# A speech joint network on one core: a leading tile of 330 outputs, weight sums over PSUM and on GpSimd, and orders found anew

## The chip, the cores and the metric

The kernel runs on one core of one Trainium2 chip. The metric is the device time in microseconds. TensorE (PE) does the matmuls and writes PSUM, which has eight banks of 512 fp32 columns; VectorE (DVE) and ScalarE (ACT) read and write SBUF and PSUM; GpSimd (POOL) works on SBUF here; SyncE (SP) issues nearly all transfers.

## The reference

x is 2 x 4000 x 512 in bf16, the two convolutions have 5 taps of 512 x 512, g is 2 x 8 x 512.

```python
h = sum(einsum("btc,cd->btd", xp[:, i:i+T, :], w1[i]) for i in range(5))
h = gelu(h)[:, ::2, :]                       # 2000 rows a batch
f = sum(einsum("btc,cd->btd", hp[:, i:i+T1, :], w2[i]) for i in range(5))
f = gelu(f)[:, ::2, :]                       # 1000 rows a batch
fe, ge = f @ w_f, g @ w_g
j = tanh(fe[:, :, None, :] + ge[:, None, :, :])
return einsum("btud,dv->btuv", j, w_o)       # 2 x 1000 x 8 x 512
```

Only every second output of each convolution is needed.

## The kernel before

**The stages.** Outputs of conv1 are made in two ways. The first ones of batch 0, the *leading tile*, are made directly: for each of the 5 taps, the 4 blocks of 128 input channels and the 4 blocks `m` of 128 output channels one matmul (`direct`, 80 in all) over `2 * NA` columns. It needs x transposed: the first rows of x are loaded as they are (`xr`), transposed on TensorE against an identity (`turn`) and copied to SBUF (`xs`) by ScalarE and VectorE. Eight matmuls on zeros run ahead of that.

All other outputs are made in *triples*: a fast algorithm that makes three outputs in 9 products where the direct way takes 15. A triple over `n` columns makes 3n outputs with 9 x 4 x 4 = 144 matmuls of n columns. Its products are named `t2`, `tm`, `sm`, `t1`, `s1`, `t0`, `s0`, `ti`, `si`. Batch 0 has two triples of conv1 (`N3`, 266 columns each), batch 1 two of 334, and conv2 one of 334 for each batch. The inputs of a triple are the six phases of x (every sixth row, transposed by the transfer itself, `load_x6`, to `xq` and `xp`), doubled (`d0`, `d1`, `d2`) and subtracted from each other (`r0` to `r2`, and the steps that bear the products' names) in `Triple.step`. A `Unit` is one triple's work for one block `m`: `s1` to `s5` are the products with their copies and sums.

The triples need sums of the taps' weights. `w1part` makes them for conv1, per block `m`: `t = w0 + w4`, `v = t - w2`, `u = 4 w4 + w0 + 2 w2`; `u/3` and `v/3` go to `w1_x` (for `t2` and `tm`), `t + w2` to `w1_t` (for `t1`), and `w1 - w3`, `w1 + w3`, `2 w1` (for `sm`, `s1`, `s0`) for two blocks at a time. The sums are fp32 tiles in SBUF (`ssum`); VectorE adds, ScalarE scales.

After the convolutions come `w_f`, `w_g`, the tanh on ScalarE and the joint product with `w_o` in 15 rounds (`Seven`: seven products of halved blocks for eight), with copies out of PSUM (`evict`), sums before them (`Seven.sums`, on VectorE or GpSimd) and stores.

**The order of the work.** Each operation is recorded with its engine, its tiles and a cost (`Plan.op`); `Plan.flex` records one that either of two engines can do. The order of each engine's operations is written out in `ORDER`, two characters an operation, and this also settles which engine does a flexible one. `Plan.edges` derives from the tiles who waits for whom; across engines these are semaphore waits. Each engine works strictly in its order, so what waits holds up all behind it.

**The transfers.** SP issues `xr`, then the taps 0 and 4 in parts, 2, 1 and 3, then six transposing loads for each triple. Some weight loads wait until an earlier load has landed (`gate`, an index into `came`).

The helpers record every operation, so the profile has their lines: `tt` (L398), `act` (L404), `mm` (L412), `stt` (L518), `turn` (L496, L505), `load_w` (L430), `load_x6` (L445), `load_w1` (L458), `evict` (L834, L835), `Seven.sums` (L903), `shared` (L1009).

Of the kernel before, what the change touches and what calls it, by code (L numbers as in the profile page):

```python
# [12 lines left out]
P = 128  # L13
# [50 lines left out]
class Op:  # L64
# [18 lines left out]
        "PyPePfPzQMP-Q0Q3Q4QNQCQDQIQJQFQGQPQQQTQUQXQYQbQeQfQi"),
    "act": (
        "080h0m1U0r1x1W1a1z1Z251Y2b1q271K2m1L2M1-1j2U1t2x1l1M1O332d2R1N3E2g2f2X2u2_3Z3B3H3R2h3h413c2r3K3s3M4K3x3f4C4V3p3y3w38"
        "494F4b3m3W3v4i5V5D464t4Y4P4S4y4d5C574q4w5z5B4n6E5A5g5154685d6V6g786j6v6G6M6a5j65795S6B5a745T627I7A7b6d7s5x7z7T717N6_"
        "7W7j7m5q6T7Q5w778D8d7u7g828O8B886s6t7p6S8X8-8L858o8Y9A8W9G8I8R8i8l9N7G948r9I976m9b9V9D9e9S8z9p9_9rA69YAcAXA8AFAtAdAP"
        "AfAMAeAhASAnBOAVB8BuB9AgBgCFCECs9wB7CGCqB-CJC2CCCrCDCeCwChDQCtDPDRFJDDD-CpE0DGDgEaDnFHCXEbE3D6FxFFFGFID_FwEMEFEZEPGS"
        "FyEpFNF2FYFKG_FCF5FhFzIWFkG-GIGVFvI0IVJ2GpGRGgGsHDJVH2J_HXI2IYHMHPI6I1IXIaJ-IMICIjJ6IdJ3ItI3IZJMIwJWJZK_JfK2JpKTJsNN"
        "KILSKdKRK-KnL2KUKyKqLwL8LVLILRLlL_NqKSLxM4MTMEMwMtMjMHKzMQNsN0MPMmNDNLNRMsOPNhNwNXNkNtNMOfOMNOODNrOpP6OLOiPJOoP9PPPZ"  # L90
        "PkQBPcPqP_Q1QOQHQRQgQdQk"),
    "dve": (
        "000j0o0p1R1S1v1T1V1X231w1u212Z1_1y24221b2a261d1c1Q1e1g1f1P1h1i1k28202p1m2P2Y362c1n2Q2q372e1o302i2k2j2-3U3I3V313J3L3k"
        "3P3z3l3O3N4H3-444I3_4N454Z4l4G4m4a4O4c4-4f4e504g5m5E5G5F5k5Y6D6J6F6C5l5Z5P6Y6l6L6K6Z605Q615N5O5t5p6I7C6H7D7Y6y7B5R5u"
        "6z7L7M7Z6P7q5o7X6Q5r7E6k5s5v7r7e6N806O7t7f6R816p7v6n7w6o6q7x6r8G7F8H8b8g8Z8h8u928t939H8a9F9h9f9Q9l9j9R9g8s9k9J9E9i9n"
        "9y9K9-A09mADA3A7AAA1AEAJ9uAHAOAL9vB5B69LAkAYAZBPAbAuBQAvBCAqA_BjBVBIBFBvB1BYBcBmBLByCaBpCMCPBsCZClC8CzCbCVDUCSD0CWD8"
        "DkDXEyEGEzEHD3DqDMDaE6DdDyDuEqDzEtErGCE9EkECEeEvFbEwEVEhEnFEF9FQExGjFtG6G0FTFaFWG3FqGBG9GYGLGbGPGiHHIGHlHIGyGeHFH5Hi"
        "HBHdH8HkHrHaHgHTI9H_HuIHIoJGIPIFITIgJHIpImJCJ9J0JcJFJjKDJkJiJPJTK5JyKXK8KBKaKgKPKLKjKkLDM8KwLbLfM9L5LBLPLuLYLLM1LeLo"
        "M7MAMBMdN4MLMZMWMzNAMqMcNHNUN3OZNdNbO4NcO5NaO3NzNoOAOVO0OsOSOyOvOHOmPDOYO-PMP2PTPuP3PUPvPSPnPgPtQ5QEQKQVQZQcQj"),
    "pool": (  # L100
        "01020304050s0t0u2A0v0w0x295n8VAaBSAwBRAxBwCYDjBxD9D7DhDiE-DAE_EJEsEIFcEuFeGkFdGlGDHGGFGEHmIIGmHoHJHnJIInIqIJJJKCJlKF"
        "KhKEJmLCKiLFLgLELiLhMfMeN5MgN6N7NeO6O7OaOcObP0P1PWPVPwPx"),
    "sp": (
        "0607090A0B0C0D0E0F0G0H0I0J0K0L0M0N0O0P0Q0R0S0T0U0V0W0X2B2C2D2E2F2G2H2I2J2K5H5I5J5K5L5M8S8T8UB2BZBdC3C4C5C9CiCmDHDIDJ"
        "DNDrDvEQERESEWF6FAFlFmFnFrGMGQGtGuGvGzHQHUHvHwHxH-IQIUIxIyIzJ1JQJUJtJuJvJzKMKQKrKsKtKxLMLQLpLqLrLvMIMMMNMOMnMrNENINJ"
        "NKNlNpOEOIOJOKOjOnPAPEPFPGPdPhQ2Q6Q7Q8QLQSQWQaQh"),
# [178 lines left out]
def bass_standalone__seq2seq_rnn_t_joint__speech_kernel(  # L285
# [25 lines left out]
    NA, N3 = 204, (266, 266)  # L311
# [9 lines left out]
    with ExitStack() as es:  # L321
# [33 lines left out]
        xq = [Buf(nc, f"xq{i}", [6, NK, (288, 288)[i]], BF16, v.end - v.bytes) for i, v in enumerate((xs[1], w2_sb))]  # L355
# [108 lines left out]
        def load_xq(i, ph):  # L464
            o = load_x6(xq[i], 0, ph, 2 * NA // 3 + i * N3[0] - 2, 0, -(-(N3[i] + 3 - i) // 16) * 16)
            if (i, ph) in ((0, 4), (0, 0)):
                o.wire = 1.050 if ph else 2.520

        lo, hi, al = slice(0, 2), slice(2, NK), slice(0, D)
        for i, part, gate in ((0, (lo, al), None), (0, (hi, al), None), (4, (slice(0, NK), slice(0, D // 2)), None),  # L470
                              (4, (slice(0, NK), slice(D // 2, D)), 0), (2, None, 1), (1, None, 3), (3, None, 5)):
            load_w1(i, part, gate)
        for ph in (4, 0, 2, 1, 3, 5):
            load_xq(0, ph)
# [14 lines left out]
        def turn(rt, pp, rs, bk):  # L489
# [8 lines left out]
            pl.op("pe", fn, (xr[rt].rows(0, n), ident[:]), (pv,), k * (0.2 if rt else 0.275))  # L498
# [41 lines left out]
        w13 = {0: 2, 2: 4}  # L540

        def w1part(m, part):
            sl = slice(m * P, (m + 1) * P)
            w = lambda i: w1_sb[i, :, sl]
            if part == "s":
# [8 lines left out]
                stt("dve", u, w(2), 2.0, u)  # L554
                act(w1_x[1, :, sl], u, ACT.Copy, scale=1.0 / 3.0)
                tt("dve", v, t, w(2), sub)
                act(w1_x[0, :, sl], v, ACT.Copy, scale=1.0 / 3.0)
                tt("dve", w1_t[2, :, sl], t, w(2), add)
# [3 lines left out]
        class Triple:  # L562
# [14 lines left out]
            def step(self, which):  # L577
                z, r = self.z, self.r
                E = self.n + 2
                if which[0] == "d":  # L580
                    i = int(which[1])
                    act(r(i, n=E), z(2 * i - 2, 0, E) if i else z(4, -1, E), ACT.Copy, scale=2.0)
# [3 lines left out]
                elif which == "next":  # L586
                    act(z(3), r(0, 1), ACT.Copy)
                elif which == "prev":
                    act(z(2), z(5, -1), ACT.Copy)
# [17 lines left out]
        class Unit:  # L607
# [15 lines left out]
            def s1(self):  # L623
                self.A = banks.pop(0)
                self.t.product("t2", self.m, self.A, True)
                act(self.c, self.pa(), ACT.Copy, scale=1.5)

            def s2(self):
                self.t.product("tm", self.m, self.A, False)
                self.t.product("sm", self.m, self.A, False)  # L630
                act(self.s, self.pa(), ACT.Copy, scale=-1.0)
# [46 lines left out]
        memset(xq[1][0:4, :, 1 + N3[1]:4 + N3[1]])  # L678
        memset(xq[1][4:6, :, N3[1]:4 + N3[1]])
# [102 lines left out]
        w1part(0, "s")  # L782
        for w in STEPS:
            trip[0].step(w)
        for m in range(1, NK):
            when((0, 0, 1)[m - 1], lambda m=m: w1part(m, "s"))
# [219 lines left out]

        def shared(o, x, y, op, pool):
            pl.port = True
            fn = lambda e: e.tensor_tensor(out=o.ap, in0=x.ap, in1=y.ap, op=op)  # L1009
            n = o.ap.free_size()  # L1010
            pl.flex({"dve": (fn, 0.065 + 0.52e-3 * n), **({"pool": (fn, 0.02 + 2.14e-3 * n)} if pool else {})}, (x, y), (o,))
            pl.port = False
# [223 lines left out]
```

## Time and profile before

| | |
|---|---|
| median of 3 runs | 249.01 us (248.55 to 249.67) |
| profiled execution: span from the first to the last instruction | 247.2 us |
| instructions | 5277 |
| first matmul, first of the leading tile | 1.19 us, 7.37 us |
| first product of the first triple | 19.86 us |
| last instruction on TensorE ends | 244.11 us |
| HBM read, written | 7.66 MB, 16.38 MB |

Of the profiled execution the page gives the span; what lies around it is the rest up to the time of a run. In a row of the profile stand line, engine, operation, what it writes and reads, the shapes and how often, then the busy time in us and the mean of one in ns, then the idle time of the engine just before, with what ended it. In the timeline a row begins with its start and its length in us.

### The profile page before, as it was taken

What the parts mean: (1) busy time and instruction counts of PE and PEld (TensorE: products, weight loads), DVE (VectorE), ACT (ScalarE), POOL (GpSimd) and SP (SyncE); (2) the same over time, 40 slices, a digit from 0 to 9 for tenths busy, and PEclk for the clock granted to TensorE, in tenths of its full rate; (3) what the DMA queues carried; (4) which work ended last, traced back from release to release, by engine and by line L of the source; (5) the groups of instructions that cost most, each with busy time, mean ns of one, the idle gap of its engine ahead of it and who ended that gap; (6) DMA issues with size and microseconds to landing.
All of it is one profiled execution on the core that took longest, in us unless ns stands there. A gap on an engine that the chain in (4) does not pass through costs nothing.

```text
span 247.2 us, 5277 instructions
## 1 busy us (share of the span) xinstructions
PE 242.8 (98%) x1932; PEld 186.1 (75%) x1932; DVE 224.8 (91%) x403; ACT 210.7 (85%) x359; POOL 83.8 (34%) x90
## 2 busy tenths in 40 slices
PE   8999999999999999999999999999999999999995
PEld 4657888877666666666567888778788888888883
DVE  1799998867999999699998999999999999999994
ACT  3269799899669857986799999999999999999992
POOL 1000000000000000000015584677887886796861
PEclk9999999999999999999999999999999999999999
DMA  6998999997700340000000234413433655356377
GB/s 215 331 193 168 185 157 205 150 177 174 254 2 3 119 135 3 1 1 3 0 0 3 85 102 139 143 48 129 131 127 103 195 171 172 132 187 200 123 258 233
DMA packets 57890, 31.87 MB, mean 129 GB/s; under 512 B 33835, under 2 KB 57659, under 8 KB 57865
## 3 DMA queue, kind: packets, MB, share of 16 engines
q1 hardware_dynamic: 57577, 31.41, 48.5%
q8 instruction: 15, 0.25, 0.4%
q10 hardware_dynamic: 288, 0.13, 0.2%
q14 instruction: 10, 0.08, 0.1%
HBM read 7.66 MB, written 16.38 MB: 97 GB/s over the span
## 4 chain that ended last, share of the span: by engine, by line
PE 98%; DVE 0%; issue 0%
PE acc L412 97%; PE acc L496 1%; DVE ost L835 0%; DVE xs L505 0%; DVE zero L419 0%
## 5 line engine op out<-in xcount | busy, mean ns | idle before, releaser
L398 DVE TENSOR_TENSOR og<-acc,sn 128x512 bf16<-128x512 f32 x93 | 60.0, 690 | 1.9 <-PE acc L412 1.2
L412 PE MATMUL acc<-tw,ss 128*128 128x256 f16 x372 | 58.0, 273 | 0.0
L404 ACT ACTIVATE jT<-feT,geT 128x1000 bf16<-128x1000 f32 (+6 forms) x56 | 53.2, 1002 | 1.8 <-DVE feT L398 1.5
L834 ACT ACTIVATE sn<-acc 128x512 f32<-128x512 f32 (+1 forms) x70 | 43.0, 707 | 1.0 <-PE acc L412 0.7
L412 PEld LDWEIGHTS acc<-tw,ss 128*128 128x128 f16 x372 | 36.0, 98 | 6.5 <-ACT sn L834 0.2
L903 POOL TENSOR_TENSOR ss<-jT 128x512 f16<-128x512 bf16 x24 | 27.7, 1168 | 25.0 <-DVE feT L398 22.5
L412 PE MATMUL acc<-row,w_sb 128*128 128x334 bf16 (+1 forms) x192 | 31.7, 296 | 0.0
L412 PE MATMUL acc<-wo_sb,jT 128*128 128x256 bf16 x176 | 29.2, 273 | 0.0
L404 ACT ACTIVATE sd<-acc 128x334 f32<-128x334 f32 (+1 forms) x48 | 20.6, 435 | 10.1 <-PE acc L412 9.6
L412 PE MATMUL acc<-row,w_x 128*128 128x266 bf16 (+1 forms) x192 | 28.4, 291 | 0.0
L404 ACT ACTIVATE jX<-feT,geT 128x1000 bf16<-128x1000 f32 (+4 forms) x28 | 27.4, 1042 | 0.0
L394 POOL MEMSET hT<- 128x8 bf16 (+2 forms) x6 | 0.7, 149 | 70.5 <-ACT hT L404 70.5
L412 PEld LDWEIGHTS acc<-row,w_sb 128*128 128x128 bf16 x192 | 18.7, 98 | 6.3
L412 PEld LDWEIGHTS acc<-row,w_x 128*128 128x128 bf16 x192 | 18.7, 98 | 5.7
L903 POOL TENSOR_TENSOR ss<-jT,ss 128x512 f16<-128x512 bf16 x14 | 16.6, 1189 | 15.1 <-DVE ss L903 9.7
L412 PE MATMUL acc<-wo_sb,ss 128*128 128x256 bf16 x124 | 21.0, 273 | 0.0
L412 PEld LDWEIGHTS acc<-wo_sb,jT 128*128 128x128 bf16 x176 | 17.2, 98 | 3.1
L835 DVE COPY sn<-acc 128x512 f32<-128x512 f32 (+1 forms) x25 | 16.8, 691 | 1.1 <-PE acc L412 1.0
L412 PE MATMUL acc<-hT,w_sb 128*128 128x334 bf16 x96 | 17.1, 305 | 0.0
L518 DVE SCALAR_TENSOR_TENSOR acc<-acc,sd 128x334 f32<-128x334 f32 (+1 forms) x24 | 11.7, 487 | 5.8 <-PE acc L412 5.6
L404 ACT ACTIVATE hT<-acc 128x266 bf16<-128x266 f32 (+2 forms) x36 | 14.6, 433 | 2.7 <-PE acc L412 2.4
L834 ACT ACTIVATE og<-acc 128x512 bf16<-128x512 f32 x22 | 15.3, 710 | 1.5 <-PE acc L412 1.5
(113 smaller groups left out, 502.5 us busy)
## 6 DMA issues: line engine op xcount, KB each, us to landing
out_dram<-og SPq DMA_DIRECT2D x45, 256.0 KB, 2.3
w_sb<-in_w_dram SPq DMA_DIRECT2D x8, 512.0 KB, 4.9
out_dram<-og SPq DMA_DIRECT2D x19, 128.0 KB, 2.2
w_sb<-in_w_dram SPq DMA_DIRECT2D x4, 256.0 KB, 4.8
xr<-in_x_dram SPq DMA_DIRECT2D x1, 512.0 KB, 3.5
wf_sb<-in_w_f_dram SPq DMA_DIRECT2D x1, 512.0 KB, 3.6
wg_sb<-in_w_g_dram SPq DMA_DIRECT2D x1, 512.0 KB, 5.1
wo_sb<-in_w_o_dram SPq DMA_DIRECT2D x1, 512.0 KB, 5.2
```

The lines of the kernel that those rows point to most:

```text
L394: pl.op("pool", lambda e: e.memset(v.ap, 0.0), (), (v,))
L398: pl.op(eng, lambda e: e.tensor_tensor(out=o.ap, in0=a.ap, in1=b.ap, op=op), (a, b), (o,), 0.02 + 2.14e-3 * o.ap.free_size() if eng == "po ...
L404: pl.op("act", lambda e: e.activation(o.ap, i.ap, func, scale=scale, bias=0.0 if bias is None else bias.ap), rd, (o,), o.ap.free_size() * ...
L412: ins = e.matmul(o.ap, lhsT=l.ap, rhs=r.ap, start=start and n == 0, stop=stop and n == len(pairs) - 1, skip_group_check=not check)
L496: ins = e.transpose(pv.ap[:, i, k, :], xr[rt].h[0:n, 2 * r + pp, k, :], ident.h[0:n, 0:n])
L518: pl.op(eng, lambda e: e.scalar_tensor_tensor(out=o.ap, in0=a.ap, scalar=f, in1=b.ap, op0=ALU.mult, op1=add), (a, b), (o,), vec_cost(o, (a ...
L834: pl.flex({"act": (lambda e: e.activation(o.ap, v.ap, ACT.Copy), 0.05 + n * 0.833e-3), "dve": (lambda e: e.tensor_copy(out=o.ap, in_=v.ap) ...
L835: "dve": (lambda e: e.tensor_copy(out=o.ap, in_=v.ap), 0.065 + n * 1.04e-3)}, (v,), (o,))
L903: fn = lambda e, o=S[i], x=x, y=y, op=op: e.tensor_tensor(out=o.ap, in0=x.ap, in1=y.ap, op=op)
```

## The change

- `NA` goes from 204 to 165: the leading tile makes 330 outputs, not 408, and its second row tile of x has 39 rows, not 78. `N3` goes from (266, 266) to (240, 318). The transposing loads of these two triples have 256 and 320 columns, not 272.
- `w1part` is rewritten. For blocks 0 and 1 (home `P`) `u` and `t`, for 2 and 3 (home `G`) `u` lies in a PSUM bank (`WBANK`): ScalarE copies `w4` there, VectorE's sums read and write there. For blocks 2 and 3 GpSimd makes `t`, `v` and `t + w2`. The sums of taps 1 and 3 (`w13part`) may run on VectorE or GpSimd, and doubled taps on ScalarE or VectorE.
- The doublings and shifts of a triple and the scaled copies of a unit, so far ScalarE's, may run on either of ScalarE and VectorE (`scaled`).
- Tap 3's load waits for the first half of tap 4, not the second. Clears of `xq[1]` are made phase by phase, each behind its load.
- `ORDER` is new for all engines. By it the leading tile's 80 matmuls stand together, with no product of a triple among them; VectorE has 14 sums of 512 columns before the first triple's `t2`; GpSimd has seven sums for conv1, and two more joint sums (73, not 71).

```diff
-    NA, N3 = 204, (266, 266)
+    NA, N3 = 165, (240, 318)
...
-            load_w1(i, part, gate)
-        for ph in (4, 0, 2, 1, 3, 5):
-            load_xq(0, ph)
+        for kind, i in (('w', 1), ('w', 3), ('x', 4), ('x', 0), ('x', 2), ('x', 1), ('x', 3), ('x', 5)):
+            if kind == "w":
+                load_w1(i, None, len(came) - 4)
+            else:
+                load_xq(0, i)
...
+        WBANK = ((6, 7), (5, 4), (6, 7), (5, 4))
+        WHOME = ('P', 'P', 'G', 'G')
+
+        def scaled(o, i, f):
+            n = o.ap.free_size()
+            fast = not i.psum and o.ap.dtype == BF16 and i.ap.dtype == BF16
+            pl.port = fast
+            pl.flex({"act": (lambda e: e.activation(o.ap, i.ap, ACT.Copy, scale=f), ...),
+                     "dve": (lambda e: e.tensor_scalar_mul(out=o.ap, in0=i.ap, scalar1=f), ...)}, (i,), (o,))
...
         def w1part(m, part):
-                t, v, u = ssum[4][:], ssum[m % 2][:], ssum[2 + m % 2][:]
-                if m in w13:
-                    n = slice(m * P, w13[m] * P)
-                    act(w1_t[1, :, n], w1_sb[1, :, n], ACT.Copy, scale=2.0)
-                    tt("dve", w1_t[0, :, n], w1_sb[1, :, n], w1_sb[3, :, n], add)
-                    tt("dve", w1_x[2, :, n], w1_sb[1, :, n], w1_sb[3, :, n], sub)
-                tt("dve", t, w(0), w(4), add)
-                stt("dve", u, w(4), 4.0, w(0))
...
+            home = WHOME[m]
+            if home != "S":
+                u, t = (ps.cols(bk * NT, NT).map(...) for bk in WBANK[m])
+                act(u, w(4), ACT.Copy)
+                w4 = u
+            else:
+                t, u, w4 = ssum[4][:], ssum[2 + m % 2][:], w(4)
+            if home == "G":
+                t, v = ssum[4][:], ssum[m % 2][:]
+                tt("pool", t, w(0), w(4), add)
+                tt("pool", v, t, w(2), sub)
+                tt("pool", w1_t[2, :, sl], t, w(2), add)
+            else:
+                v = t if home == "P" else ssum[m % 2][:]
+                tt("dve", t, w4, w(0), add)
+            stt("dve", u, w4, 4.0, w(0))
+            stt("dve", u, w(2), 2.0, u)
+            act(w1_x[1, :, sl], u, ACT.Copy, scale=1.0 / 3.0)
+            if home != "G":
+                tt("dve", w1_t[2, :, sl], t, w(2), add)
                 tt("dve", v, t, w(2), sub)
+            act(w1_x[0, :, sl], v, ACT.Copy, scale=1.0 / 3.0)
+
+        def w13part(m):
+            n = slice(m * P, (m + 2) * P)
+            shared(w1_x[2, :, n], w1_sb[1, :, n], w1_sb[3, :, n], sub, True)
+            shared(w1_t[0, :, n], w1_sb[1, :, n], w1_sb[3, :, n], add, True)
+            scaled(w1_t[1, :, n], w1_sb[1, :, n], 2.0)
...
-                    act(r(i, n=E), z(2 * i - 2, 0, E) if i else z(4, -1, E), ACT.Copy, scale=2.0)
+                    scaled(r(i, n=E), z(2 * i - 2, 0, E) if i else z(4, -1, E), 2.0)
...
-                act(self.c, self.pa(), ACT.Copy, scale=1.5)
+                scaled(self.c, self.pa(), 1.5)
...
-        memset(xq[1][0:4, :, 1 + N3[1]:4 + N3[1]])
-        memset(xq[1][4:6, :, N3[1]:4 + N3[1]])
+        for ph in (4, 0, 2, 1, 3, 5):
+            memset(xq[1][ph, :, (1 if ph < 4 else 0) + N3[1]:4 + N3[1]])
```

Left out are the strings of `ORDER`, the changed cost figures, and the places where `scaled` stands for `act` in the same way.

More of the change, by code (lines that the diff above doesn't have):

```diff
@@ L354, in bass_standalone__seq2seq_rnn_t_joint__speech_kernel @@
         assert all(xp[i].end <= xs[i].end for i in xp)
-        xq = [Buf(nc, f"xq{i}", [6, NK, (288, 288)[i]], BF16, v.end - v.bytes) for i, v in enumerate((xs[1], w2_sb))]
+        xq = [Buf(nc, f"xq{i}", [6, NK, (352, 352)[i]], BF16, v.end - v.bytes) for i, v in enumerate((xs[1], w2_sb))]
         assert xq[0].end <= xs[1].end and xq[1].end <= w2_sb.end
@@ L586, in step @@
                 elif which == "next":
-                    act(z(3), r(0, 1), ACT.Copy)
+                    scaled(z(3), r(0, 1), 1.0)
                 elif which == "prev":
-                    act(z(2), z(5, -1), ACT.Copy)
+                    scaled(z(2), z(5, -1), 1.0)
                 else:
@@ L630, in s2 @@
                 self.t.product("sm", self.m, self.A, False)
-                act(self.s, self.pa(), ACT.Copy, scale=-1.0)
+                scaled(self.s, self.pa(), -1.0)
             def s3(self):
@@ L780, in steps @@
             when(slot, *[lambda w=w: trip[i].step(w) for w in STEPS[lo:hi]])
-        w1part(0, "s")
+        for m in range(NK):
+            w1part(m, "s")
+        for m in (0, 2):
+            w13part(m)
         for w in STEPS:
             trip[0].step(w)
-        for m in range(1, NK):
-            when((0, 0, 1)[m - 1], lambda m=m: w1part(m, "s"))
         when(17, load_late, lambda: tail_zero(1))
```

93 lines of the change are left out of this document (46 added, 47 removed).

## The prediction

> **What bounds the kernel now.** The page first: busy times, then the chain that ended last.
>
> ```profile
> PE 242.8 (98%) x1932; PEld 186.1 (75%) x1932; DVE 224.8 (91%) x403; ACT 210.7 (85%) x359; POOL 83.8 (34%) x90
> ...
> PE 98%; DVE 0%; issue 0%
> PE acc L412 97%; PE acc L496 1%; DVE ost L835 0%; DVE xs L505 0%; DVE zero L419 0%
> ```
>
> TensorE is busy 98% of the span, and 97% of the chain is its matmuls. So columns fed to TensorE and new waits of TensorE decide; no other engine's time counts by itself. Then busy time by stage (length, PE, PEld, DVE, ACT, POOL):
>
> ```profile
> 7.37:23.05 15.68, 15.68 (x97) 9.33 (x97) 14.71 (x25) 9.48 (x17) 0.00 (x0) 1.00 1.02 229
> ...
> 120.00:240.00 120.00, 120.00 (x1018) 98.48 (x1017) 116.71 (x218) 117.83 (x189) 80.25 (x70) 1.00 0.38 123
> ```
>
> While TensorE works on the leading tile (7.37 to 23.05) it never idles, GpSimd does nothing, and VectorE, at 14.71 of 15.68 us, prepares the first triple. TensorE's timeline there:
>
> ```profile
> 7.37 12.65 PE L412 MATMUL acc<-xs,w_sb 128*128 128x408 bf16 x72
> 19.86 1.98 PE L412 MATMUL acc<-row,w_x 128*128 128x266 bf16 x16
> 21.67 1.54 PE L412 MATMUL acc<-xs,w_sb 128*128 128x408 bf16 x8
> 23.05 1.18 PE L412 MATMUL acc<-row,w_x 128*128 128x266 bf16 x9
> ```
>
> From start to start, 8 matmuls of 408 columns take 23.05 - 21.67 = 1.38 us, 0.1725 each; 16 of 266 take 21.67 - 19.86 = 1.81 us, 0.113 each. That is 0.000417 us a column. The triple's first four products (`t2`, x16) start at 19.86, but before the next (`tm`, from 23.05) stand eight leading matmuls: 1.38 us of cover for VectorE.
>
> **The change, part by part.**
>
> *Columns.* The leading tile's 80 matmuls lose 78 columns: -6240. The first triple's 144 lose 26: -3744. The second's 144 gain 52: +7488. Net -2496 columns x 0.000417 = **-1.04 us**. By the same line a matmul of 330 columns takes 0.140 us, of 240 0.102, of 318 0.135.
>
> *Start.* The second row tile has 39 rows, not 78. The leading tile starts when VectorE's copy of it ends:
>
> ```profile
> L496 PE MATMUL acc<-ident,xr 78*128 78x78 bf16 x16 | 0.9, 228 | 0.0
> 6.99 0.92 DVE L505 COPY xs<-acc 128x312 bf16<-128x312 bf16 x2 [0.89 <-PE acc L496]
> ```
>
> Half of the 0.9 us of these transposes is 0.45, the upper bound; zero is the lower, if a short transpose costs what a long one does. I take **-0.15 us**, from the halved copy alone: the leading tile starts at 7.2.
>
> *Weight sums.* VectorE's and ScalarE's rows:
>
> ```profile
> 10.77 0.69 DVE L518 SCALAR_TENSOR_TENSOR ssum<-w_sb,ssum 128x512 f32<-128x512 bf16 x1 [0.88 <-DMA w_sb<-in_w_dram]
> 11.38 0.69 DVE L398 TENSOR_TENSOR ssum<-ssum,w_sb 128x512 f32<-128x512 f32 x1
> 11.98 0.69 DVE L398 TENSOR_TENSOR w_t<-ssum,w_sb 128x512 bf16<-128x512 f32 x1
> ...
> 18.00 0.72 DVE L398 TENSOR_TENSOR row<-xq 128x1064 bf16<-128x1064 bf16 x1
> 18.62 0.69 DVE L518 SCALAR_TENSOR_TENSOR ssum<-w_sb,ssum 128x512 f32<-128x512 bf16 x1
> ...
> 13.90 1.15 ACT L404 ACTIVATE w_x<-ssum 128x512 bf16<-128x512 f32 x2 [1.20 <-DVE ssum L518]
> ...
> 17.45 1.08 ACT L404 ACTIVATE row<-xq 128x1072 bf16<-128x1072 bf16 x1
> ```
>
> A 512-wide sum takes 0.60 us start to start, a 1064-wide bf16 one 0.62; 960 wide I take 0.57. In the changed order VectorE has 14 sums of 512 before `t2`, all with an operand in PSUM; GpSimd takes six others and one 1024-wide one. For a PSUM operand the page has:
>
> ```profile
> L398 DVE TENSOR_TENSOR og<-acc,sn 128x512 bf16<-128x512 f32 x93 | 60.0, 690 | 1.9 <-PE acc L412 1.2
> L903 POOL TENSOR_TENSOR ss<-jT 128x512 f16<-128x512 bf16 x24 | 27.7, 1168 | 25.0 <-DVE feT L398 22.5
> ```
>
> 690 ns against 690 from SBUF: PSUM costs the same. But ten of the 14 now read and write the same bank, which no row shows. Lower bound 0; upper, if reading and writing take turns, another 0.53 us (the 512 elements once more: 0.60 less a fixed 0.07, since 0.62 for 1064 elements at two a step and 0.60 for 512 at one both fit it). I take 0, as in the PSUM row.
>
> The chain begins with two new copies of tap 4's weights to PSUM on ScalarE, which wait for that tap's first half:
>
> ```profile
> L458 SPq DMA_DIRECT2D w_sb<-in_w_dram x1: 469/469/469, 2.6 to 2.6; - x1
> DMA to landing us min/median/max: 5.3/5.3/5.3
> ...
> L445 SPq DMA_TRANSPOSE xq<-in_x_dram x12: 1309/1618/2555, 9.2 to 28.1; - x12
> ...
> L445 SPq DMA_TRANSPOSE xq<-in_x_dram x1: 2555/2555/2555, 11.0 to 11.0; - x1
> DMA to landing us min/median/max: 6.1/6.1/6.1
> ...
> L445 SPq DMA_TRANSPOSE xq<-in_x_dram x1: 1312/1312/1312, 13.6 to 13.6; - x1
> DMA to landing us min/median/max: 4.6/4.6/4.6
> ```
>
> It landed at 2.6 + 5.3 = 7.9. The row tile ahead of it is 156 KB shorter, at the 229 GB/s of the stage row 0.7 us; I take 0.5, so 7.4. The copy takes 0.63 (the ScalarE row): VectorE begins at 8.1. Fourteen sums, 14 x 0.60 + 0.1 for one sum that waits for its neighbour: 16.6. `t2` needs the second transpose of x (17.1 before; 16.3 after, as it starts earlier and has 256 columns for 272), so VectorE is later: `t2` 16.6 to 17.2. TensorE ends the leading tile at 7.2 + 80 x 0.140 = 18.4 and goes straight on with `t2`: no wait there.
>
> *The wait this adds.* The next four products, `tm`, follow without cover: 18.4 + 16 x 0.102 = **20.0**. VectorE does, after `t2`: `r0`, one 1024-wide difference (0.60), `r1`, `r2`, `tm`: 4 x 0.57 + 0.60 + 0.1 = 2.98, plus 0.1 until the write is seen: 17.2 + 3.1 = **20.3**. `r2` also waits for ScalarE's third doubling; ScalarE can take the last unit's scaled sum when VectorE has it, near 16.2, then two doublings: 16.2 + 0.5 + 2 x 0.98 (968 elements of 1072 in 1.08): 18.7, before VectorE gets there at 19.0; the data of that doubling lands by 17.5 (13.6 + 4.6 = 18.2 before). So TensorE waits some **+0.35 us**, with every later matmul behind it. What follows is covered, thinly. `sm`: VectorE at 20.3 + 0.60 + 0.57 = 21.5, TensorE at 20.35 + 12 x 0.102 = 21.6. GpSimd's last sum is queued behind two clears that wait for the second triple's first two transposes: 12 issues in 9.2 to 28.1 are 1.72 each for 272 columns, so 16.3 + 4 x 1.62 + 2 x 2.02 = 26.8, and 1.3 for the sum: 28.1. Its product (the 25th group of four after `t2` begins) comes at 20.35 + 20 x 0.41 = 28.6.
>
> *GpSimd.* Its chain starts with the second half of tap 4 (8.5: 256 KB more at 229 GB/s); the second sum waits for tap 2 (10.7 before, VectorE's DMA wait; 10.2 now), and `v` of the fourth unit is the sixth unit of 1.15 us from there: 17.1. ScalarE reaches its copy near 19.3, after the doublings. Spare: 2 us. Its rows are f16; f32 is unseen: I take 1.15, bounds 1.15 and twice that.
>
> One rule of the chip speaks against this part. Rows first:
>
> ```profile
> 164.82 1.53 POOL L903 TENSOR_TENSOR ss<-ss,jT 128x512 f16<-128x512 f16 x1 [1.47 <-DVE ss L903]
> 166.31 1.15 POOL L1009 TENSOR_TENSOR fs<-wf_sb,fs 128x512 f16<-128x512 bf16 x1
> ...
> 164.66 0.68 DVE L1009 TENSOR_TENSOR ft<-fT 128x1008 bf16<-128x1008 bf16 x1
> 165.25 2.06 DVE L398 TENSOR_TENSOR og<-acc,sn 128x512 bf16<-128x512 f32 x3
> ```
>
> A GpSimd sum that meets a VectorE sum with two SBUF inputs takes 0.38 us longer; beside one with a PSUM operand, none. The Trainium skill (GPSIMD Engine Reference, section 8, Key points) says that GpSimd shares its SBUF interfaces with VectorE and contends with instructions that have two SBUF inputs; the trace agrees. Here the 14 sums are safe, and GpSimd's `v` (16.0 to 17.1) meets `t2` at 16.6: if VectorE is the one held, `tm` comes 0.38 later.
>
> *Copies on either engine, orders.* In the listing of the changed program, doublings and scalings move from ScalarE to VectorE and GpSimd has two more joint sums. Both engines stand behind TensorE; I cost it at nothing. The cover is thin: 116.71 and 117.83 of 120 us busy.
>
> **Sum.** -1.04 - 0.15 + 0.35 = -0.84 us. The profiled span is 247.2 us; the median of the runs is 249.01, 1.8 more lies around the span and stays. So 249.01 - 0.84 = **248.2 us** (span 246.4).
>
> **Rivals.**
>
> 1. *No wait.* The loads come as much earlier as the bytes allow and the shorter transposes give their full 0.45: -1.04 - 0.45 = -1.5, 247.5 us. For: VectorE misses by a third of a microsecond only. Against: 14 sums in a row leave nothing to catch up with.
> 2. *`t2` late by 0.4*: GpSimd holds VectorE, or the transposes land as late as before. -0.84 + 0.38: 248.6 us.
> 3. *Slower: same-bank sums in PSUM.* Ten sums at +0.53 end the chain 5.3 later, and TensorE waits for `t2` and `tm` by 5.6 in all: -1.19 + 5.6 = +4.4, 253.4 us. It decides from 0.08 us a sum on (10 x 0.08 + 0.35 eats up the 1.19); at 0.21 the kernel is 0.5% slower. For: no row has such an operand pair. Against: PSUM operands in different banks cost nothing.
> 4. *Slower: the new order of the joint stage.* If each of its 15 rounds waits 0.2 us, +3.0: 251.2 us. For: both engines are 97% busy there. Against: TensorE's 120.00 of 120 us with the same work.
>
> That the change doesn't do what it says is no rival: the listing has the column counts.
>
> **How the numbers follow.** Forecast 0.43, rival 1 0.25, rival 2 0.12, rival 3 0.11, rival 4 0.09. 0.5% (1.25 us) is about what a measurement can tell from no change, so the forecast is inside it. Faster by more than that: most of rival 1 and the fast edge of the forecast, 0.25. Slower: rivals 3 and 4 and a little more, 0.21. Within: 0.54. The range takes in rival 1, the forecast and rival 2 with the runs' own spread (248.55 to 249.67 is 0.6 either way): 246.9 to 250.0; rivals 3 and 4, 0.20, stay outside.
>
> **What would show it.** The leading tile's row x80 of 330 columns starting near 7.2 and `t2` at 18.4; VectorE's sums 0.60 apart though in PSUM; an idle time of TensorE of 0.2 to 0.5 us near 20 with VectorE's `row` as releaser, and none over 0.2 later; GpSimd's sums at 1.15. Wrong: PSUM sums over 0.7 apart, ScalarE waiting for GpSimd before 20 us, or gaps of TensorE after 120 us adding up to over 1 us.

## The result, and the profile after

The changed kernel takes 251.52 us (median of 6 runs, 250.44 to 252.31), the kernel before 248.69 (248.55 to 249.67): a ratio of 1.0108, interval 1.0093 to 1.0123. It is slower by 1.1%, or 2.8 us, where 248.2 was forecast, and outside the range. (Of the kernels further down, c3_five and c2_nogate each had one execution, for c2_nogate the profiled one, that took 425.6 and 425.9 us at a granted clock of 0.56; no ratio counts these.) The profiled execution has a span of 250.1 us, 2.9 more than before. The page of the changed kernel, busy times and the chain that ended last:

```profile
PE 241.8 (97%) x1932; PEld 184.3 (74%) x1932; DVE 229.7 (92%) x409; ACT 201.3 (80%) x348; POOL 95.5 (38%) x103
...
PE 84%; DMA 6%; DVE 3%; SPq 2%; ACT 2%; issue 1%; DVEq 0%
```

TensorE has 1.0 us less to do (242.8 to 241.8), as the columns said, and yet the span grew: the chain, 98% TensorE before, now runs for 13% through transfers, VectorE, SP and ScalarE. Where that is, busy time by stage tells (length, PE, PEld, DVE, ACT, POOL), first the kernel before, then the changed one:

```profile
10.00:20.00 10.00, 10.00 (x60) 5.64 (x59) 9.23 (x16) 6.43 (x10) 0.00 (x0) 1.00 1.02 222
20.00:30.00 10.00, 10.00 (x87) 8.16 (x85) 9.99 (x18) 8.50 (x17) 0.22 (x2) 1.00 0.96 176
...
160.00:180.00 20.00, 20.00 (x159) 15.32 (x158) 19.61 (x36) 19.93 (x34) 13.98 (x12) 1.00 0.35 115
```

```profile
10.00:20.00 10.00, 9.25 (x68) 6.31 (x66) 9.12 (x16) 7.46 (x12) 6.92 (x7) 1.00 1.15 216
20.00:30.00 10.00, 8.64 (x81) 7.76 (x82) 9.82 (x21) 6.75 (x16) 1.87 (x7) 1.00 0.98 189
...
160.00:180.00 20.00, 19.34 (x155) 14.70 (x153) 19.93 (x35) 19.57 (x32) 14.34 (x13) 1.00 0.35 116
```

TensorE's waits lie in three places: 10 to 30 us, 160 to 180, and a third one at 240. Its timeline in the changed kernel:

```profile
6.37 11.47 PE L413 MATMUL acc<-xs,w_sb 128*128 128x330 bf16 x80
18.45 1.41 PE L413 MATMUL acc<-row,w_x 128*128 128x240 bf16 x12 [0.61 <-DVE row L399]
20.18 0.58 PE L413 MATMUL acc<-row,w_x 128*128 128x240 bf16 x4 [0.33 <-ACT w_x L405]
21.55 2.62 PE L413 MATMUL acc<-row,w_x 128*128 128x240 bf16 x24 [0.79 <-ACT hT L405]
...
28.66 0.58 PE L413 MATMUL acc<-row,w_sb 128*128 128x240 bf16 x4 [0.39 <-DVE acc L522]
...
174.17 0.60 PE L413 MATMUL acc<-ft,wf_sb 128*128 128x504 bf16 x2 [0.24 <-DVE ft L589]
...
175.41 0.39 PE L413 MATMUL acc<-wo_sb,jT 128*128 128x256 bf16 x2 [0.42 <-DVE og L399]
...
241.18 0.39 PE L413 MATMUL acc<-tw,jT 128*128 128x256 f16 x2 [0.69 <-DVE og L399]
```

A matmul's end is modelled, so the brackets are a little short. From the start of one matmul to the next, less what its columns take back to back, the seven waits are 0.77, 0.49, 0.95, 0.55, 0.41, 0.58 and 0.85 us: 4.6 in all. The balance of the span is then: columns -1.04, the leading tile's start 7.37 - 6.37 = -1.00, waits +4.6, and the last 3.3 us behind TensorE's last start, which became 3.7, +0.4; together +3.0, against the +2.9 of the span.

VectorE in the changed kernel, at the places that TensorE waits for, and GpSimd beside it:

```profile
15.60 1.28 DVE L522 SCALAR_TENSOR_TENSOR acc<-w_sb,acc 128x512 f32<-128x512 bf16 x2
17.73 0.66 DVE L399 TENSOR_TENSOR row<-xq 128x960 bf16<-128x960 bf16 x1 [0.84 <-DMA xq<-in_x_dram]
...
20.75 0.66 DVE L399 TENSOR_TENSOR row<-row 128x960 bf16<-128x960 bf16 x1
...
26.98 1.29 DVE L399 TENSOR_TENSOR row<-row,xq 128x960 bf16<-128x960 bf16 x1
...
172.45 1.67 DVE L589 TENSOR_TENSOR ft<-fT,ft 128x1008 bf16<-128x1008 bf16 x1
...
240.43 0.69 DVE L399 TENSOR_TENSOR og<-acc,sn 128x512 bf16<-128x512 f32 x1 [1.05 <-DMA out_dram<-og]
```

```profile
26.45 1.32 POOL L399 TENSOR_TENSOR w_t<-ssum,w_sb 128x512 bf16<-128x512 f32 x1
...
172.42 1.15 POOL L938 TENSOR_TENSOR ss<-jT,ss 128x512 f16<-128x512 bf16 x1
173.53 1.59 POOL L938 TENSOR_TENSOR ss<-jX 128x512 f16<-128x512 bf16 x1
```

To be seen: the 14 sums end at 16.9 (forecast: 16.6), and then VectorE itself waits 0.84 us for the second transpose of x, which lands at 17.71. The input of `tm` is ready at 20.75 + 0.66 = 21.41. The view puts TensorE's wait there down to ScalarE's `hT`, which ends at 21.52, but what ends it is VectorE's `row`. In all eleven traces with a wait ahead of `tm`, TensorE starts 0.15 us after that `row` has ended, and in six of them before `hT` has ended, as in c2_four, one of the kernels further down (`row` ends at 20.53, `hT` at 20.86, TensorE starts at 20.68):

```profile
19.87 0.66 DVE L407 TENSOR_TENSOR row<-row 128x960 bf16<-128x960 bf16 x1
20.39 0.47 ACT L413 ACTIVATE hT<-acc 128x330 bf16<-128x330 f32 x1
20.68 2.62 PE L421 MATMUL acc<-row,w_x 128*128 128x240 bf16 x24 [0.36 <-DVE row L407]
```

At 26.98 and 172.45 two of VectorE's sums take 1.29 and 1.67 us; both began while a GpSimd sum was under way, 0.54 and 0.03 us after its start. At 240.43 a sum waits for a store to land, to reuse its buffer.

How far the sum at 172.45 is out of the ordinary, the group of VectorE's sums `ft` shows (ns, least/median/most):

```profile
L589 DVE TENSOR_TENSOR ft<-fT,ft x4: 674/680/1665, 118.2 to 172.4; 128x1008 bf16<-128x1008 bf16 x4
```

### The profile page after: what moved, and what is told of

Its sections match the earlier page's. It is cut to its first block, busy times and chain, and to the rows that moved or that the text cites. A ratio compares the mean times of both kernels' runs of the same rounds, so it can differ in the third digit from the quotient of the medians.

```text
span 250.1 us, 5277 instructions
## 1 busy us (share of the span) xinstructions
PE 241.8 (97%) x1932; PEld 184.3 (74%) x1932; DVE 229.7 (92%) x409; ACT 201.3 (80%) x348; POOL 95.5 (38%) x103
## 4 chain that ended last, share of the span: by engine, by line
PE 84%; DMA 6%; DVE 3%; SPq 2%; ACT 2%; issue 1%; DVEq 0%
PE acc L413 84%; DMA xq<-in_x_dram 2%; DMA w_sb<-in_w_dram 2%; DMA out_dram<-og 2%; SPq L446 1%; DVE feT L399 1%; ACT row L551 1%; DVE row L399 1%; DVE og L399 1%; DVE acc L522 0%; ACT w_x L405 0%; SPq L459 0%; SPq L439 0%; DVE sn L874 0%; ACT og L869 0%
## 5 line engine op out<-in xcount | busy, mean ns | idle before, releaser
L405 ACT ACTIVATE jT<-feT,geT 128x1000 bf16<-128x1000 f32 (+6 forms) x56 | 51.5, 979 | 0.1
L869 ACT ACTIVATE sn<-acc 128x512 f32<-128x512 f32 (+1 forms) x68 | 40.3, 666 | 3.2 <-PE acc L413 3.1
L938 POOL TENSOR_TENSOR ss<-jT 128x512 f16<-128x512 bf16 x20 | 22.9, 1155 | 29.9 <-ACT jT L405 26.2
L413 PE MATMUL acc<-row,w_sb 128*128 128x334 bf16 (+2 forms) x192 | 32.6, 297 | 0.4 <-DVE acc L522 0.4
L413 PE MATMUL acc<-row,w_x 128*128 128x334 bf16 (+2 forms) x192 | 30.4, 294 | 1.7 <-ACT hT L405 0.8
L551 ACT ACTIVATE sd<-acc 128x334 f32<-128x334 f32 (+2 forms) x39 | 16.6, 432 | 17.0 <-PE acc L413 16.7
L413 PEld LDWEIGHTS acc<-row,w_x 128*128 128x128 bf16 x192 | 18.5, 98 | 8.4 <-ACT hT L405 1.0
L413 PE MATMUL acc<-wo_sb,ss 128*128 128x256 bf16 x124 | 22.4, 273 | 0.0
L938 POOL TENSOR_TENSOR ss<-jT,ss 128x512 f16<-128x512 bf16 x15 | 17.9, 1195 | 8.4 <-DVE ss L938 8.3
L938 POOL TENSOR_TENSOR ss<-ss,jT 128x512 f16<-128x512 f16 x14 | 16.6, 1193 | 10.3 <-DVE ss L938 7.5
L405 ACT ACTIVATE hT<-acc 128x334 bf16<-128x334 f32 (+3 forms) x36 | 15.0, 433 | 6.2 <-PE acc L413 6.0
L413 PE MATMUL acc<-row,w_t 128*128 128x334 bf16 x96 | 16.6, 305 | 0.0
```

The costliest lines, as they stand in the source:

```text
L405: pl.op("act", lambda e: e.activation(o.ap, i.ap, func, scale=scale, bias=0.0 if bias is None else bias.ap), rd, (o,), o.ap.free_size() * ...
L413: ins = e.matmul(o.ap, lhsT=l.ap, rhs=r.ap, start=start and n == 0, stop=stop and n == len(pairs) - 1, skip_group_check=not check)
L551: pl.flex({"act": (lambda e: e.activation(o.ap, i.ap, ACT.Copy, scale=f), n * 0.833e-3 + (0.05 if i.psum else 0.105)), "dve": (lambda e: e ...
L869: pl.flex({"act": (lambda e: e.activation(o.ap, v.ap, ACT.Copy), 0.05 + n * 0.833e-3), "dve": (lambda e: e.tensor_copy(out=o.ap, in_=v.ap) ...
L938: fn = lambda e, o=S[i], x=x, y=y, op=op: e.tensor_tensor(out=o.ap, in0=x.ap, in1=y.ap, op=op)
```

## The experiments

Each kernel is the changed one with the edit shown. Ratios are to the kernel before, run beside it (248.8 to 248.9); the changed kernel's is 1.0108. In the orders, operations are written by name. The name of each kernel stands at its measured time.

### The order ahead of tm

```diff
 VectorE:
+  w1-w3 (first half; was GpSimd's)
   t2
+  d2 (was ScalarE's)
-  r0, w1-w3 (second half)
   r1, r2, tm, sm
+  w1-w3 (second half), r0
   w1+w3, t1, s1
 GpSimd:
   t (block 3)
+  v, t+w2 (block 3)
```

> The changed kernel with the order of the first 28 us mended, nothing else: the doubling d2 on VectorE and not on ScalarE, the first half of w1 - w3 on VectorE ahead of t2 and not on GpSimd, GpSimd's last sum right behind the one before it, and r0 and the second half of w1 - w3 behind tm and sm. Theory A (the idle times at 19.6, 20.5 and 28.0 us come from what the new order queues ahead of tm, and from a GpSimd sum that holds up VectorE): tm's input is ready at 20.7 and not 21.4; idle times 0.49 and 0.95 become one of some 0.6, the 0.55 at 28.0 goes; 251.5 - 1.4 = 250.1. Rival B (VectorE simply has too much to do there, so what is moved back is missed later): new idle times between 22 and 30 us of the same sum, 251.5.

Measured (e2_early): 251.23 us, ratio 1.0107 (1.0075 to 1.0139). TensorE's waits in it:

```profile
18.45 1.81 PE L421 MATMUL acc<-row,w_x 128*128 128x240 bf16 x16 [0.56 <-DVE row L407]
20.70 2.62 PE L421 MATMUL acc<-row,w_x 128*128 128x240 bf16 x24 [0.43 <-ACT hT L413]
23.64 2.73 PE L421 MATMUL acc<-xq,w_t 128*128 128x240 bf16 x24 [0.32 <-ACT sd L559]
```

`tm` came at 20.70 and not 21.55, and then a new wait of 0.49 us ended at 23.64, and others of 0.31 at 26.5 and 0.19 at 36.6. This was rival B: between 17.7 and 28 us VectorE's rows follow one another without a gap, and what is taken from the front of its queue is missed behind.

### The load of tap 3

```diff
-                load_w1(i, None, len(came) - 4)
+                load_w1(i, None, len(came) - (4 if i == 1 else 3))
```

> The changed kernel with one line undone: tap 3's load waits for the second half of tap 4 again, as before the change. Changed kernel: 251.5 us, xq's second transposing load landed at 17.71, TensorE idle 0.77 us ahead of t2 at 17.54. Theory A (the earlier start of tap 3 and of the transposing loads behind it makes them share the transfer engines and all land later): that load lands near 17.0, the idle time ahead of t2 shrinks to some 0.2 us, the time falls by about 0.5 us to 251.0. Rival B (the bytes ahead set the landing, not when they are issued): it lands at 17.7 or later, the time stays within 0.2 us of 251.5.

Measured (e1_gate): 250.66 us, ratio 1.0072 (1.0050 to 1.0094); the second transposing load landed at 16.16. That looked like theory A; the pair of four edits below, where the same line changed nothing, does not bear it out.

### The sizes of before in the new order

```diff
-    NA, N3 = 165, (240, 318)
+    NA, N3 = 204, (266, 266)
```

> The changed kernel, its orders and engines, with the sizes of before: a leading tile of 408 outputs and triples of 266 and 266. By columns alone it is 2496 x 0.000417 = 1.04 us slower, 252.6. Theory A (in the new order the start of t2 and tm is set by the transposes of x and by VectorE's queue, not by the leading tile, so that the columns taken from the leading tile only turned into waiting): the leading tile ends near 20.5, with no idle time of TensorE before tm and under 0.5 us until 40 us, and the time is 250.5 to 251.5, no slower than with the new sizes. Rival B (the waits come with the queues whatever the sizes): waits of 2 us and more before 40 us as in the changed kernel, 252.6.

Measured (e5_sizes): 251.47 us, ratio 1.0107 (1.0089 to 1.0126): the same time, with 2496 more columns.

```profile
6.56 14.02 PE L421 MATMUL acc<-xs,w_sb 128*128 128x408 bf16 x80
20.41 4.70 PE L421 MATMUL acc<-row,w_x 128*128 128x266 bf16 x40
24.94 2.88 PE L421 MATMUL acc<-xq,w_t 128*128 128x266 bf16 x24
```

`t2`, `tm` and `sm` go through in one row of 40 with no wait. Until 40 us TensorE waits 0.4 us where the changed kernel waits 2.8; it then meets new waits of 1.0 us between 51 and 59, 0.8 of them at 53.5. The order was made for the other sizes; that this is the reason is likely but not shown. Against the changed kernel the balance is columns +1.04, waits ahead of 40 us -2.4, the new ones +1.0, at 241 us +0.2, the start +0.2: 0.1 us in all, and the spans are equal. Theory A: the columns taken from the leading tile had been the cover for VectorE's queue, and came back as waiting. It also shows where the loss comes from. With the sizes of before, everything else in the change (orders, weight sums, loads) loses 2.6 us against the kernel before (251.47 to 248.87); the new sizes neither add to it nor take from it.

### GpSimd's last sum of weights

```diff
 GpSimd: clear, clear,
-  t+w2 (block 3),
   clear, clear, clear,
+  t+w2 (block 3),
```

> The changed kernel with one instruction moved: GpSimd's last sum of weights (w_t of the fourth block), which ran at 26.4 beside VectorE's ti, stands three clears later, near 28. Theory A (it held ti up by 0.65 us, and the idle time of 0.55 at 28.0 is that): ti takes 0.65, the idle time at 28.0 goes, 251.5 - 0.5 = 251.0. Rival B (VectorE's queue is what is late, and the sum will hold up another one): an idle time of 0.4 or more between 27 and 31 us stays, 251.5.

Measured (e6_sum119): 250.30 us, ratio 1.0057 (1.0035 to 1.0080). VectorE's rows:

```profile
26.20 0.40 DVE L530 SCALAR_TENSOR_TENSOR acc<-acc,sd 128x240 f32<-128x240 f32 x1
26.52 0.65 DVE L407 TENSOR_TENSOR row<-row,xq 128x960 bf16<-128x960 bf16 x1
```

`ti` takes 0.65 us where it took 1.29, and TensorE has no wait between 21.1 and 40 us: one instruction, moved by three clears, takes away a wait of 0.55 us. The time fell by more, 1.2 us or 0.5% (1.0108 less 1.0057). In the traces the rest lies where the edit changes nothing: the leading tile starts 0.21 us sooner, and TensorE waits 0.25 less ahead of `tm` and 0.27 less at 240. So the edit is worth some 0.2%, and the rest is how these executions fell out.

### The sum ft away from a GpSimd sum

```diff
 VectorE: ft(1), ft(2),
+  ft(3),
   og, og, og, sn, og, og, feT, sn, feT, sn,
-  ft(3),
   feT
```

> The changed kernel with one instruction moved: the last of VectorE's three 1008-wide sums ft, which took 1.67 us at 172.4 beside a GpSimd sum and 0.68 elsewhere, stands right behind the other two at 166.4, where GpSimd is idle. Theory A (a VectorE sum of two SBUF operands waits until the GpSimd sum under way has ended, and the idle times of TensorE at 173.7 and 174.7, 0.41 and 0.58, are that wait passed on): the sum takes 0.68, both idle times go, 251.5 - 1.0 = 250.5. Rival B (VectorE is full there, whatever the hold): its other sums come 0.6 later, TensorE waits between 167 and 175 as long as before, 251.5.

Measured (e3_hold): 251.36 us, ratio 1.0094 (1.0074 to 1.0113).

```profile
165.45 1.40 DVE L597 TENSOR_TENSOR ft<-fT,ft 128x1008 bf16<-128x1008 bf16 x2
166.76 1.88 DVE L407 TENSOR_TENSOR og<-acc,sn 128x512 bf16<-128x512 f32 x3
```

```profile
168.10 0.39 PE L421 MATMUL acc<-tw,jT 128*128 128x256 f16 x2 [0.17 <-DVE og L407]
```

Half of each theory: the sum takes its 0.68 us and the waits at 173.7 and 174.7 are gone, but the three `og` sums behind it come 0.6 later, and TensorE waits until 168.1 (0.34 from start to start) and 171.1 (0.14). Of 1.0 us 0.5 is left. The time itself (1.0094 to 1.0108) is not clear of noise. The run c3_five below puts the same sum elsewhere.

### The store at 240 us

```diff
 VectorE: og (waits for the store),
+  (behind the next two)
 TensorE: the two matmul groups on its bank
+  (behind the next eight)
 ScalarE: their copy to og
+  (behind the next two copies sn)
```

> The changed kernel with three places changed in the last 10 us: VectorE's sum og that waited 1.05 us at 239.4 for a store to land stands behind the next two, and the two matmuls and the copy that need the bank that it frees stand behind the next eight matmuls. Theory A (the 0.85 us of TensorE at 240.2 are a store's landing time of some 2.1 us, met because the new order puts the last product of the round that used this buffer too near): that idle time goes, 251.5 - 0.8 = 250.7. Rival B (the last stores end the span, not TensorE): TensorE ends earlier but the span does not, 251.5.

Measured (e4_tail): 252.14 us, ratio 1.0126 (1.0108 to 1.0144), the slowest of all. SP's queue at its end:

```profile
243.63 0.37 SPq L994 DMA_DIRECT2D out_dram<-og  x1
244.05 1.33 SPq L892 DMA_DIRECT2D out_dram<-og  x3
245.42 0.39 SPq L1002 DMA_DIRECT2D out_dram<-og  x1
245.86 0.47 SPq L994 DMA_DIRECT2D out_dram<-og  x1
246.37 1.72 SPq L1002 DMA_DIRECT2D out_dram<-og  x3
```

TensorE's wait at 240 went (its last start is 245.31, and 246.35 in the changed kernel), but the copy that was moved back fills a buffer whose store stands early in SP's queue. From 243.6 on SP issues nine stores almost without a pause, each 0.4 to 0.6 us; the last one's data was ready at 245.88 and it was issued at 247.46. Rival B.

```diff
 VectorE: og (waits for the store),
+  (behind the next copy sn)
 TensorE: the two matmul groups on its bank
+  (behind the next four)
```

> The changed kernel, a milder change of the last 10 us than e4_tail: the sum og that waits for the store stands behind one VectorE copy only, and the two matmuls that need its bank behind four matmul groups that don't; the copies on ScalarE, and so the stores, stay in their order. Theory A (the idle time of 0.85 at 240.2 is the wait for the store, and e4_tail lost its gain because a store moved back held up SP's queue): the idle time goes, the last store is issued 0.6 us earlier, 251.5 - 0.6 = 250.9. Rival B (the last stores end the span whatever TensorE does): TensorE ends 0.8 earlier, the span stays, 251.5.

Measured (e7_tail2): 250.92 us, ratio 1.0085 (1.0072 to 1.0098): the 0.6 us expected. TensorE's wait of 0.85 became 0.18 and 0.25. So that wait was the store's landing, and the edit is worth some 0.4 us by the trace; that the time gives the full 0.6 is in part luck. In the changed kernel the two stores issued at 236.35 and 236.78 take about 4 us to land where the median of their kind is 2.3; why these, no run here tells.

### Four edits together, with and without the load's line

These are the edits of e1_gate, e3_hold, e6_sum119 and e7_tail2.

> Four edits together: e1_gate, e3_hold, e6_sum119 and e7_tail2. If the losses are separate and add, 251.5 - 0.9 - 0.2 to 0.5 - 0.5 - 0.6 = 249.0 to 249.3, with idle times of TensorE after 7 us of 1.5 us in all where the changed kernel has 5.3. If the loss is one shortage of VectorE that moves from place to place, over 250.3.

Measured (c2_four): 249.73 us (249.61 to 249.86), ratio 1.0035 (1.0023 to 1.0047). Of 2.7 us two thirds are back, and TensorE's waits add up to 1.7 us, near the 1.5 expected. The times add less well: expected were 249.0 to 249.3, and the four gains measured one by one make some 3 us, the four together 1.8. The gains of e1_gate and e6_sum119 by themselves held more than their edits.

```diff
-                load_w1(i, None, len(came) - (4 if i == 1 else 3))
+                load_w1(i, None, len(came) - 4)
```

> c2_four without its first edit: tap 3's load waits for the first half of tap 4, as in the changed kernel. c2_four took 249.73. Theory A (the earlier load costs 0.6 to 0.9 us, as the time of e1_gate says): 250.4 or more, with the wait ahead of tm over 0.9 us. Rival B (what e1_gate gained was the chance of its landings, since in c2_four the second transposing load landed at 16.83 in spite of the gate): within 0.2 us of 249.73.

Measured (c2_nogate): 249.91 us, ratio 1.0035 (1.0022 to 1.0048): rival B. In the traces with the line the first transpose is issued at 8.7 to 9.5 us and the second lands at 16.2 to 16.9 (in c5_sizes186, where the first taps landed 1.5 us later than elsewhere, at 10.5 and 18.3); in those without it, at 8.0 to 8.4 and 16.5 to 17.7. (What the wait ahead of `tm` was in c2_nogate was not seen.) So an issue of the first load that is up to 1.5 us earlier brings no earlier landing of the second. SP's rows show why, the changed kernel's first, then those of the kernel before:

```profile
L446 SPq DMA_TRANSPOSE xq<-in_x_dram x2: 2608/3028/3447, 8.0 to 11.5; - x2
L445 SPq DMA_TRANSPOSE xq<-in_x_dram x2: 1695/2125/2555, 9.2 to 11.0; - x2
```

In the changed kernel SP began to issue the first load at 7.99 and took 3.45 us for it, before 1.70 from 9.24 on. So the second was issued at 11.48, not 10.98, and landed 6.2 us after that (before: 6.1). The other traces of loads of 256 columns fit: from 7.99 the first takes SP 2.7 to 3.5 us, from 8.3 on 2.0 to 2.3, from 8.7 on 1.4; the second is issued at 10.1 to 10.9 in all but the changed kernel's, and lands 5.9 to 6.7 us later. What e1_gate gained stays open: the two times of this pair say that the line costs nothing.

### The sum ft at a better place, and one copy moved

```diff
 VectorE: ft(1), ft(2),
-  ft(3),
   og, og, og, sn, og, og, feT, sn,
+  ft(3),
   feT, sn, feT
 ...
-  sn (ahead of the og that waits for the store; now ScalarE's)
```

> c2_four with two places changed: the moved 1008-wide sum stands ahead of the feT sum at 171.2, where a GpSimd sum is just ending, and not at 166.4, where it made three og sums 0.6 later; and the copy sn on VectorE at 238.2, ahead of the sum that waits for the store, is ScalarE's, which is idle there. Expected if both waits are VectorE's queue: the idle times at 166.6 and 169.7 (0.33 and 0.14) go, and of 0.32 and 0.25 at 239.3 and 241.2 most; VectorE ends 0.5 earlier: 249.73 - 1.0 = 248.8. If VectorE is short everywhere: 249.7.

Measured (c3_five): 249.48 us, ratio 1.0022 (1.0011 to 1.0034). VectorE, GpSimd and the stage:

```profile
170.12 0.67 DVE L597 TENSOR_TENSOR ft<-fT,ft 128x1008 bf16<-128x1008 bf16 x1
```

```profile
169.09 1.16 POOL L946 TENSOR_TENSOR ss<-ss,jT 128x512 f16<-128x512 f16 x1
170.20 1.61 POOL L946 TENSOR_TENSOR ss<-jT 128x512 f16<-128x512 bf16 x1
```

```profile
160.00:180.00 20.00, 20.00 (x160) 15.36 (x159) 19.97 (x37) 20.00 (x34) 14.87 (x13) 1.00 0.36 120
```

Here VectorE comes first, at 170.12, takes its 0.67 us, and it is GpSimd that waits (1.61 us). TensorE is busy for 20.00 of 20 us again, as in the kernel before: GpSimd had the time to spare, VectorE did not. In these traces the loss of this stage hung on which of the two began first. The other half gave less: in the profiled execution a wait of 0.62 us until 239.8 was still there. So 0.25 us came of the 1.0 expected; waits of 1.7 us ahead of `tm`, where c2_four's trace has 0.5, took back what the stage gave in this execution.

### Sizes in between

```diff
-    NA, N3 = 165, (240, 318)
+    NA, N3 = 174, (240, 312)
```

> c3_five with a size between those of before and of the change: a leading tile of 348 outputs and triples of 240 and 312. Columns by themselves: (18 x 80 - 6 x 144) x 0.000417 = +0.24 us. If the wait ahead of tm (0.5 us) is lack of cover by the leading tile: 0.24 - 0.5 = 0.26 us under c3_five. If not: 0.24 over it.

Measured (c4_sizes174): 249.19 us, ratio 1.0014 (1.0001 to 1.0027), some 0.3 below c3_five, as expected for lack of cover, but the two intervals are as wide as that. TensorE waits for `tm` still:

```profile
18.66 1.87 PE L421 MATMUL acc<-row,w_x 128*128 128x240 bf16 x16
21.22 0.98 PE L421 MATMUL acc<-row,w_x 128*128 128x240 bf16 x8 [0.68 <-DVE row L407]
```

```diff
-    NA, N3 = 174, (240, 312)
+    NA, N3 = 186, (236, 308)
```

> c4_sizes174 with a longer leading tile still: 372 outputs, triples of 236 and 308. Columns by themselves: (24 x 80 - 8 x 144) x 0.000417 = +0.32 us. The leading tile is 24 x 80 x 0.000417 = 0.80 us longer, the wait ahead of tm in c4_sizes174 was 0.85. Theory A (that wait is lack of cover): under 0.15 us of it are left and the time is 249.19 + 0.32 - 0.75 = 248.8, level with the kernel before (248.9). Rival B (VectorE's queue moves back with the leading tile): the wait stays over 0.5 us, 249.4.

Measured (c5_sizes186): 249.19 us, ratio 1.0013 (0.9998 to 1.0028). The wait ahead of `tm` shrank to 0.13 us as in theory A, but the time did not. The columns took 0.32 of the 0.72 us; where the other 0.4 went is open, and the two intervals (some 0.3 us either way each) can hide it. The profiled execution, the slowest of its twelve, is no clean witness: its first taps landed late, and leading tile and VectorE's queue both began 1.2 us later than in c4_sizes174. No version here is faster than the kernel before; the best two are within 0.15% of it.

## Why the prediction was wrong, step by step

**Columns: right.** -1.04 us; TensorE's busy time fell by 1.0.

**Start: right in size, but not what the trace shows.** -0.15 was taken, with 0.45 as the bound. The shorter row tile's 16 transposes take 0.6 us where they took 0.9, inside the bound. In the profiled execution the leading tile starts 1.00 us earlier, but 0.6 of that is the first row tile's 16 transposes, which the change leaves alone (before, then changed):

```profile
L496 PE MATMUL acc<-ident,xr 128*128 128x128 bf16 x16 | 1.9, 314 | 0.0
L500 PE MATMUL acc<-ident,xr 128*128 128x128 bf16 x16 | 1.2, 229 | 0.0
```

They take from 1.1 to 1.9 us from one trace to another, whatever the kernel: 1.1 in e5_sizes, which has the sizes of before and starts at 6.56, and 1.9 in e4_tail, which has the new ones and starts at 7.13, 0.24 ahead of the kernel before. Why, no run here tells. In the traces of a leading tile of 330 it begins between 6.16 and 7.21. That proved worth little: `t2` starts between 17.9 and 18.5 in all of them.

**Weight sums: right.** The sums in PSUM stand 0.60 apart, as the one at 15.60 shows (1.28 us for two), so reading and writing one bank costs nothing: rival 3 is dead. The chain ends at 16.9 (16.6 forecast), GpSimd's fp32 sums take 1.15 to 1.16 us.

**The wait this adds: the step that failed first.** It was put at 0.35 us. In the profiled execution it is 2.2 us, in three pieces up to `tm`, and a fourth of 0.55 follows at 28. The length of VectorE's way from `t2` to `tm` was right (forecast 2.98; 18.39 to 21.41 is 3.02). Both its ends were off. The second transpose was to land at 16.3 "as it starts earlier", and landed at 17.71: the first load's issue began earlier, but held SP's queue so long that the second was issued later than before. So VectorE's `t2` ended at 18.39 and not at 17.2. At the other end TensorE was done with the leading tile at 17.7 and not at 18.4. The two ends moved apart by 1.2 + 0.7 = 1.9 us, no cover stood between, and 0.35 + 1.9 is the 2.2. That `t2` starts at 18.45, as forecast (18.4), has the wrong reason: TensorE had waited for it.

Half of this is this one execution's lot. In e4_tail, the same up to there, the leading tile was done at 18.4 as forecast, the second transpose had landed at 16.48, ahead of the end of VectorE's sums, and still:

```profile
18.44 1.80 PE L421 MATMUL acc<-row,w_x 128*128 128x240 bf16 x16
20.89 2.62 PE L421 MATMUL acc<-row,w_x 128*128 128x240 bf16 x24 [0.64 <-DVE row L407]
```

The wait ahead of `tm` is 0.81 us there, 0.46 over the forecast. That is how much later than 8.1 VectorE's first sum begins (8.56): tap 4's first half landed at 7.84 and not at 7.4, near the 7.97 of the kernel before, so that the "0.5" for the shorter row tile did not come. The sum also left out that the last group of `t2` needs ScalarE's copy of GpSimd's `v`. By its own figures that copy ends at 19.3 + 0.6 = 19.9, and TensorE gets there at 18.4 + 12 x 0.102 = 19.6; in the profiled execution this is the piece of 0.49, which the wait for `tm` would have held in any case. The step had the mechanism, and e5_sizes shows how large it is: with the old sizes the waits ahead of 40 us are 2.4 us shorter, which is more than the -1.04.

**GpSimd's neighbour: the mechanism was named, with the wrong victim.** The prediction's rows showed a GpSimd sum lengthened by 0.38 us beside a VectorE sum, and priced rival 2 by that. It put GpSimd's last sum at 26.8 to 28.1 and asked when its own product comes, but not which VectorE sum it would meet there. The traces show the other direction to be the dear one: a VectorE sum of SBUF operands that begins under a GpSimd sum waits until that one ends. In the changed kernel eight of VectorE's instructions are lengthened so, by 3.2 us in all; in the kernel before, two, by 0.25. Two of the eight reached TensorE with more than 0.2 us: `ti` (0.55 us, gone in e6_sum119) and `ft` (1.0 us, gone in c3_five). The Trainium skill (SBUF — State Buffer, "SBUF: two separate sides") says that the port pair which VectorE and GpSimd share is an exclusive lock, held for a whole instruction by whichever starts first; the trace agrees, in both directions: 1.67 us for VectorE at 172.45, 1.61 for GpSimd at 170.20 in c3_five.

**Copies on either engine, new orders: "at nothing" was 1.8 us.** This is the sum's second failed term. 1.0 us of it is `ft` at 172.4, 0.85 the wait for a store at 240. The cover had been called thin, and rival 4 gave 251.2 us, near the 251.5 measured, but by a wait in each of 15 rounds; in truth most rounds ran without one, and two places lost it all, so that its nearness is luck. The prediction's own sign for being wrong, waits after 120 us that add up to over 1 us, is what came. Another 0.4 us, the longer way from TensorE's last start to the end, was in no term.

**Rival 1** (no wait) fell. **Rival 2** named `t2` late by landings "as late as before" or by GpSimd, at 0.38 us. In the profiled execution the landing was later even than before (17.71 to 17.05), and GpSimd was done when `t2` began. In two others GpSimd's `v` held `t2` as the prediction had feared, by 0.26 us in c3_five and 0.48 in e6_sum119:

```profile
16.79 1.13 DVE L407 TENSOR_TENSOR row<-xq 128x960 bf16<-128x960 bf16 x1
```

## What to carry to other kernels

Work that is taken from the bottleneck in a place where other queues are being filled is not a gain but lost cover: price the wait by both ends, the moment the bottleneck is free and the moment its data lands, and take a landing from where loads landed before, in more than one execution, not from when the first of them will be issued. A new order needs its collisions looked for one by one, since a single instruction that starts a few hundredths of a microsecond after its rival for a port can cost more than a change of a thousand columns gives. And moving an instruction to the back of one queue moves whatever waits in order behind it, stores included.

## What the runs showed of the hardware

- VectorE's sums with an operand in PSUM don't feel GpSimd: of the 93 `og` of the changed kernel's trace 72 began under a GpSimd sum and 21 did not, with medians of 679 and 681 ns and 692 as the longest of both. Sums with both operands in SBUF do, by a plain rule: each of the eight that were lengthened took as much longer as the GpSimd sum had still to run, less 0.13 to 0.14 us (a sum of 512 columns that takes 416 ns took 932 with 0.65 us to run, 731 with 0.45, 473 with 0.19), and eight that began in a GpSimd sum's last 0.14 us took no longer. A doubling of 1024 columns from SBUF, one operand only, took 0.98 us under a GpSimd sum (e5_sizes at 26.86) and 0.42 elsewhere.
- VectorE adds into a PSUM bank that it reads at 0.60 us for 512 fp32 columns, as in SBUF.
- The time that SP takes to issue one transposing load of 256 columns went from 1.4 us to 3.5, the longer the earlier it began, and the next load's issue and landing moved with it: two runs that both issued the first at 7.99 issued the second at 10.67 and 11.48, and it landed at 16.7 and 17.7.
